# MoE 1's in products of three quarters as seven products of sums instead of eight, and its out sums kept in DRAM

## The chip, the cores and the metric

The kernel runs on one core of one Trainium2 chip, in one launch. The time is that of the device in microseconds (us). The kernel before took 873.6 us as the median of 3 runs (872.93 to 874.16).

## The reference

Three stages follow each other: a masked attention (4 batches, 8 heads, 576 positions of 64), a mixture block called MoE 1 here, and a second one, MoE 2. Both blocks work on 2304 tokens of 512 numbers.

```python
x = attention(q, k, v)                    # 2304 x 512
h = x @ w_in                              # MoE 1: 512 x 2048
g = h * tanh(log1p(exp(min(h, 20))))      # "Mish"
x = g @ w_out                             # 2048 x 512
s = silu(x @ w_gate) * (x @ w_val)        # MoE 2: 512 x 1536 each
out = s @ w_out2                          # 1536 x 512
```

All arrays are float32. The weights reach the kernel as 64-bit floats and are turned into 32-bit ones on the chip.

## The kernel before, in words

**Products.** Each operand of a product is held as a high part and a rest (`split_hi` on ScalarE makes the first, `split_lo` on VectorE or GpSimd the second). `mm3` (L130) then issues three TensorE matmuls for one product of 128 x 128 weights and 512 columns: high by high, high by rest, rest by high. All matmuls of the blocks therefore show line L132.

**Stages.** The tokens lie in five chunks: four of 512 and one of 256 (`CHUNKS`). MoE 1 cuts its 2048 inner columns into four quarters (`NQ`) of four column groups (`QF`). A step n is one quarter of one chunk: 48 matmuls make h (`g1_mm`), ScalarE takes Mish out of PSUM (`act_a`), `g_hi` and `g_lo` split it, and 48 matmuls make the part of the output that this quarter gives (`g2_mm`). `y_out` on VectorE adds that part to the chunk's sum in SBUF (`acc`, L602; the first quarter copies it, L600). The string `ORDER` is a hand-written order of attention and of the first steps of MoE 1; from step 3 on the loop at L880 issues the in products of step n and then the out products of step n - 1.

**Weights.** Each weight tile is one unit of conversion: a load into one of two `raw` buffers, a Square on ScalarE, four VectorE operations (L256 to L265), a high part on ScalarE and a rest on VectorE. `W1_STEP` and `W2_STEP` say how many units of MoE 1 and MoE 2 go into each step. Units of MoE 2 are written to DRAM (`wd_...`) and loaded again when their round comes (`ld`). 22 of its 60 units are converted in the rounds of MoE 2 itself, one VectorE operation after each product (`w_late_step`), as `LATE_ROUND` gives them out.

**MoE 2.** It already uses sums: `PROD` lists seven products per pair of chunks in place of eight (a 2 x 2 scheme of Strassen's kind). `operand` makes the sums and differences of the token side, units S12 and S34 those of the weights. A round (`c_round`) does the seven products for gate and value: three go through a copy to SBUF (ScalarE, L714), three are added to those copies (VectorE, L717), and the last is read from PSUM. There are twelve such rounds, six for each pair of chunks; `c4_round` does the small chunk and `d_tile` the out products.

**Queues.** Each engine works through its own queue in order. SyncE (SP) issues nearly all DMAs, GpSimd (POOL) none; an issue that waits holds up those behind it.

Of the kernel before, what the change touches and what calls it, by code (L numbers as in the profile page):

```python
# [104 lines left out]
def local_strided_attention__mish_moe__swiglu_kernel(  # L105
# [14 lines left out]

    def split_hi(eng, hi, src):
# [8 lines left out]
    def mm3(o, wh, wl, xh, xl, first, last, more=False):  # L130
        for lhs, rhs, i in ((wh, xh, 0), (wh, xl, 1), (wl, xh, 2)):
            nc.tensor.matmul(o, lhsT=lhs, rhs=rhs, start=first and i == 0, stop=last and i == 2, skip_group_check=more)  # L132
# [15 lines left out]
    w1list = []  # L148
    for q in range(NQ):
        w1list += [(("i", q * QF + f), w1[q * QF + f, :, 0]) for f in range(QF)]  # L150
        w1list += [(("o", q * QF + f), w1[q * QF + f, :, 1]) for f in range(QF)]
# [7 lines left out]
    n1 = len(w1list) - sum(W1_STEP.values())  # L159
    wlist, w1list = w1list[:n1], w1list[n1:]  # L160
    for n in range(3, NQ * NCH):
        k1, k2 = W1_STEP.get(n, 0), W2_STEP.get(n, 0)
        part = w2list[:k2] if n % NCH == NCH - 1 else []
        wlist += part + w1list[:k1] + ([] if part else w2list[:k2])
        del w1list[:k1], w2list[:k2]
    assert not w1list and len(w2list) == sum(LATE_ROUND)
# [45 lines left out]

    def w_ops():
# [5 lines left out]
        if len(key) == 2:  # L219
            t = sb.tile([128, 512], I32, tag="wtmp", name="wtmp", bufs=2)  # L220
            w = sb.tile([128, 2, 512], F32R, tag="w", name="w", bufs=10)
            wt[key] = w
        else:
            t = sb.tile([128, 512], I32, tag="pt", name="wt2", bufs=6)
            tag, n = (("ws", "v")[i % 2], 2) if i < late["first"] else ("w", 10)
            w = sb.tile([128, 2, 512], F32R, tag=tag, name="ws", bufs=n)
        tf = t.bitcast(F32)
        if src is None:
            t0, t1 = (f32[key[:2] + (x,)] for x in ("W0", "W1"))
            f32[key] = tf  # L230
            lo, hi = slice(0, 256), slice(256, 512)

            def s1():
                if key[2] == "S12":
                    nc.vector.tensor_tensor(out=tf[:, lo], in0=t1[:, lo], in1=t1[:, hi], op=ALU.add)
                else:
                    nc.vector.tensor_tensor(out=tf[:, lo], in0=t0[:, lo], in1=t1[:, lo], op=ALU.subtract)

            def s2():
                if key[2] == "S12":  # L240
                    nc.vector.tensor_tensor(out=tf[:, hi], in0=tf[:, lo], in1=t0[:, lo], op=ALU.subtract)
                else:
                    s = f32[key[:2] + ("S12",)]
                    nc.vector.tensor_tensor(out=tf[:, hi], in0=t0[:, hi], in1=s[:, hi], op=ALU.subtract)
                wpend.append((key, w, tf))

            return [s1, s2]
# [32 lines left out]
    def w_unit():  # L280
        w_lo(nc.vector)
        w_hi()
        for do in w_ops():
            do()

# [21 lines left out]

    def w_done():
        if any(len(x[0]) == 2 for x in wpend + whalf):
            w_flush(0, nc.vector)  # L310

# [48 lines left out]
    def at_qk(s):  # L360
        b, first, g, part = steps[s]
        w = 64 if first else LK
        sc = [ps.tile([128, 512], F32, tag="sc", name="sc", bufs=2) for _ in range(2)]
# [71 lines left out]
    def at_tr(s, half):  # L435
# [8 lines left out]
        if src:  # L444
            src = [pt[:, x:x + y].rearrange("p j k -> p (j k)") for x, y in src]
            tps[s, half] = tp = ps.tile([128, 512], F32, tag="xp", name="tp", bufs=2)[:src[0].shape[1], :128 * len(src)]
            for x, a in enumerate(src):
                nc.tensor.transpose(tp[:, 128 * x:128 * x + 128], a, ident)  # L448
# [10 lines left out]
    def at_pv(s):  # L459
        b, first, g, part = steps[s]  # L460
        n = len(part) // 2
        banks = [ps.tile([128, 512], F32, tag="tp", name="xp", bufs=1)]
        if first:
            banks.append(ps.tile([128, 512], F32, tag="xp", name="xq", bufs=2))
# [70 lines left out]
    def g1_open(n, f):  # L535
        h_ps[n, f] = ps.tile([128, 512], F32, tag="mm", name="h", bufs=3)

    def g1_mm(n, f, kc):
        q, c = divmod(n, NCH)
        t, x = (q * QF + f, kc) if q else (f // 2 + kc // 2 * 2, f % 2 * 2 + kc % 2)  # L540
# [38 lines left out]
    def g2_mm(n, y, e, f):  # L579
# [10 lines left out]
            f == 0,  # L590
            f == QF - 1,
        )

    def y_out(n, y, e):
        q, c = divmod(n, NCH)
        nt = CHUNKS[c][1]
        if q == 0:
            if e == 0:
                new_acc(c, 4, nt)
            nc.vector.tensor_copy(acc[c][:, e], y)  # L600
        else:
            nc.vector.tensor_tensor(out=acc[c][:, e], in0=acc[c][:, e], in1=y, op=ALU.add)  # L602
        if q == NQ - 1 and c == NCH - 1:
            if e == 0:
                yh[c] = sb.tile([128, 4, nt], F32R, tag=f"xh{c}", name=f"yh{c}")
                yl[c] = sb.tile([128, 4, nt], F32R, tag=f"xl{c}", name=f"yl{c}")
            split_hi(nc.scalar, yh[c][:, e], acc[c][:, e])
            split_lo(nc.gpsimd, yl[c][:, e], acc[c][:, e], yh[c][:, e])

    PS4 = [("sc", 2), ("sc", 2), ("xp", 2), ("xp", 2)]  # L610

    def g2_by_f(n, after, banks=PS4):
        nt = CHUNKS[n % NCH][1]
        y = [ps.tile([128, 512], F32, tag=t, name="y", bufs=k)[:, :nt] for t, k in banks]
        for f in range(QF):
            for e in range(4):
                g2_mm(n, y[e], e, f)
            after(f)
        for e in range(4):
            y_out(n, y[e], e)  # L620
# [31 lines left out]

    ws = {}
# [15 lines left out]
    PROD = [  # L669
        ("X", "W0", 0, "B11"),  # L670
        ("Z", "S12", 0, "T1"),
        ("X", "S12", 1, "T2"),
        ("Z", "S34", 1, "B22"),
        ("X", "S34", 0, "T3"),
        ("Y", "W0", 1, "B21"),
        ("X", "W1", 1, "T4"),
    ]
    BANK = {"g": {"X": ("mm", 3), "Y": ("mm", 3), "Z": ("mm", 3)}, "v": {"X": ("sc", 2), "Y": ("xp", 2), "Z": ("tp", 1)}}
# [14 lines left out]
    def c_round(r, between):  # L693
# [3 lines left out]
        for n, (x, a, half, b) in enumerate(PROD):  # L697
            o = ops[P][b]
            for k in "gv":
                if x not in bank[k]:  # L700
                    tag, nb = BANK[k][x]
                    bank[k][x] = ps.tile([128, 512], F32, tag=tag, name="c" + x + k, bufs=nb)
# [34 lines left out]
    def c4_round(r):  # L737
# [3 lines left out]
        for f in range(2):  # L741
            for k in "gv":
                p = ps.tile([128, 512], F32, tag=("sc", "xp")[k == "v"], name="c4", bufs=2)[:, :nt]
# [13 lines left out]
    DB = [("sc", 2), ("xp", 2), ("mm", 3), ("sc", 2), ("xp", 2), ("mm", 3), ("mm", 3), ("tp", 1)]  # L757
    db = [0]

    def d_tile(r, lc, t):  # L760
# [3 lines left out]
        tag, nb = DB[db[0] % len(DB)]  # L764
        db[0] += 1
        o = ps.tile([128, 512], F32, tag=tag, name="o", bufs=nb)
# [35 lines left out]
    with tc.manual_schedule():  # L802
# [3 lines left out]
        def spin(n):  # L806
            if not n:
                return
            wp = ps.tile([128, 512], F32, tag="mm", name="wp", bufs=3)
# [21 lines left out]
        NA = NQ * NCH  # L831

# [7 lines left out]
        def out_group(n, e, f):  # L840
            if f == 0:
                nt = CHUNKS[n % NCH][1]
                y_ps[n, e] = ps.tile([128, 512], F32, tag="mm", name="y", bufs=3)[:, :nt]
# [36 lines left out]
        for n in range(3, NA):  # L880
            q, c = divmod(n, NCH)
            units = W1_STEP.get(n, 0) + W2_STEP.get(n, 0)
            left = [units]

            def bg(k):
                at = (0, 0, 0, 0, 1, 2, 2, 3)[k] if n % NCH == NCH - 1 and units == 4 else units * k / 8
                while left[0] > at:
                    left[0] -= 1
                    w_unit()

            for f in range(QF):
                g1_open(n, f)
                for kc in range(4):
                    g1_mm(n, f, kc)
                act_a(n, f)
                bg(7 - f)
                if n == NA - 2 and f % 2:
                    operand(0, ("B11", "T1")[f // 2])

            def after(f):  # L900
                g_hi(n, f)
                g_lo(n, f)
                bg(3 - f)
                if n == NA - 2:
                    operand(0, ("T2", "B22", "T3", "B21")[f])
                if n == NA - 1 and f == 0:
                    operand(0, "T4")

            if n == NA - 1:
                w_flush(0, nc.vector)  # L910
                ld(0, "S34", "W0", "S12", "W1", 0, 1)
            w_done()
            g2_by_f(n - 1, after)
            w_done()
        g2_by_f(NA - 1, lambda f: None, [("mm", 3), ("mm", 3), ("mm", 3), ("tp", 1)])
        w_late()
        for r in range(2 * NP + 1):
            P = r // NP
            late["units"] += LATE_ROUND[r] if r < len(LATE_ROUND) else 0
            if r < 2 * NP:  # L920
                ld(r + 1, "W0")

                def between(n):
                    if n == 2:
# [120 lines left out]
```

## Time and profile before

| | |
|---|---|
| median of 3 runs | 873.6 us |
| span of the profiled execution, first to last instruction | 871.4 us |
| TensorE (PE) busy | 864.0 us, 99% |
| VectorE (DVE) busy | 578.4 us, 66% |
| ScalarE (ACT) busy | 383.0 us, 44% |
| GpSimd (POOL) busy | 151.0 us, 17% |

The page gives no second time for the profiled execution, so its own time is taken as its span and the 2.2 us by which the median is longer. By the chain of waits, attention with the steps 0 to 2 of MoE 1 takes 117 us, the rest of MoE 1 lasts until 457.6 us, and MoE 2 takes what is left. An engine's busy time is the union of its instructions; where instructions overlap, the mean length of one is longer than the distance from one start to the next.

### The profile page before, as it was taken

Reading aid. Unit: us, or ns where it says so; the run is one execution under the profiler, and the core shown is the slowest. Engines: PE = TensorE matmul, PEld = TensorE weight load, DVE = VectorE, ACT = ScalarE, POOL = GpSimd, SP = SyncE. Lnnn points to the kernel's source line nnn. Section 1 sums busy time; section 2 is a strip of 40 time slices with the busy share of each in tenths; the row PEclk is TensorE's granted clock in tenths of the full one; section 3 lists DMA queues with packets and bytes.
Section 4 is the critical chain, followed back from the end, with each engine's and each line's share of the span. In section 5 each row is a group of like instructions: output and inputs, shape, how many; then the busy total and the mean of one; then the engine's idle time right before and its main releaser. Section 6 shows DMA issues by size and latency. Waiting matters only on the chain.

```text
span 871.4 us, 14324 instructions
## 1 busy us (share of the span) xinstructions
PE 864.0 (99%) x5288; PEld 721.4 (83%) x5288; DVE 578.4 (66%) x1292; ACT 383.0 (44%) x971; POOL 151.0 (17%) x170
## 2 busy tenths in 40 slices
PE   8999999999999999999999999999999999999998
PEld 5788778888888888888898888888888888888886
DVE  6998756798768868695567897683455535433534
ACT  7999953344335444343435534342333322332230
POOL 5642310000000000000213321220324112111211
PEclk9999999999999999999999999999999999999999
DMA  9865314355334544241068878647150582454222
GB/s 301 269 211 166 113 60 145 99 191 194 121 120 162 201 153 156 61 163 73 0 246 309 320 297 341 236 184 284 53 194 28 200 302 95 174 193 165 83 92 97
DMA packets 46006, 149.29 MB, mean 171 GB/s; under 512 B 4976, under 2 KB 8688, under 8 KB 45936
## 3 DMA queue, kind: packets, MB, share of 16 engines
q1 hardware_dynamic: 45792, 148.16, 48.2%
q8 instruction: 42, 0.69, 0.3%
q14 instruction: 28, 0.23, 0.1%
q10 hardware_dynamic: 144, 0.21, 0.1%
HBM read 112.18 MB, written 36.18 MB: 170 GB/s over the span
## 4 chain that ended last, share of the span: by engine, by line
PE 97%; DVE 1%; ACT 0%; issue 0%; POOL 0%; POOLq 0%
PE h L132 23%; PE y L132 22%; PE o L132 17%; PE cXg L132 8%; PE cXv L132 7%; PE c L132 4%; PE cZv L132 4%; PE cZg L132 4%; PE cYv L132 2%; PE cYg L132 2%; PE sc L368 2%; PE xp L484 2%; PE tp L448 1%; DVE pt L388 1%; PE wp L811 0%; ACT pt L402 0%
## 5 line engine op out<-in xcount | busy, mean ns | idle before, releaser
L132 PE MATMUL y<-g,w 128*128 128x512 f32 (+1 forms) x960 | 203.7, 369 | 0.0
L132 PEld LDWEIGHTS y<-g,w 128*128 128x128 f32 x960 | 166.7, 189 | 29.6
L132 PE MATMUL h<-xh,w 128*128 128x512 f32 (+1 forms) x640 | 189.8, 372 | 0.0
L132 PE MATMUL o<-wr,fs 128*128 128x512 f32 x648 | 149.6, 389 | 0.0
L132 PEld LDWEIGHTS o<-wr,fs 128*128 128x128 f32 x648 | 121.3, 188 | 25.0
L132 PEld LDWEIGHTS h<-xh,w 128*128 128x128 f32 x640 | 116.4, 189 | 20.0
L132 PE MATMUL h<-xl,w 128*128 128x512 f32 (+1 forms) x320 | 117.9, 368 | 0.0
L566 ACT ACTIVATE u<-h 128x512 f32<-128x512 f32 (+1 forms) x68 | 37.3, 548 | 143.9 <-PE h L132 143.9
L128 POOL TENSOR_TENSOR fs<-k,fs 128x512 fp32r<-128x512 f32 x36 | 48.7, 1353 | 267.1 <-ACT fs L123 208.5
L776 DVE TENSOR_TENSOR acc<-acc,o 128x512 f32<-128x512 f32 x90 | 61.4, 685 | 48.7 <-PE o L132 48.6
L132 PEld LDWEIGHTS h<-xl,w 128*128 128x128 f32 x320 | 60.4, 189 | 9.5 <-DVE xl L128 0.3
L128 DVE TENSOR_TENSOR g<-u,g 128x512 fp32r<-128x512 f32 (+1 forms) x80 | 52.9, 679 | 13.6 <-ACT g L123 13.6
L128 POOL TENSOR_TENSOR B<-acc,B 128x512 fp32r<-128x512 f32 x6 | 8.3, 1391 | 307.4 <-ACT B L123 307.4
L123 ACT CAST fs<-k 128x512 fp32r<-128x512 f32 x36 | 22.4, 622 | 88.0 <-DVE k L731 37.6
L402 ACT ACTIVATE pt<-pt,sm 128x64 f32<-128x64 f32 (+1 forms) x160 | 55.9, 361 | 3.7 <-DVE sm L388 3.7
L717 DVE TENSOR_TENSOR k<-cZg,k 128x512 f32<-128x512 f32 x12 | 8.3, 692 | 72.7 <-PE cZg L132 72.7
L132 PE MATMUL cXg<-T,wr 128*128 128x512 f32 x216 | 54.8, 389 | 0.0
L132 PE MATMUL cXv<-T,wr 128*128 128x512 f32 x216 | 54.8, 389 | 0.0
L123 ACT CAST ws<-wt 128x512 fp32r<-128x512 f32 x60 | 37.0, 616 | 36.1 <-DVE wt L265 32.0
L123 ACT CAST g<-u 128x512 fp32r<-128x512 f32 (+1 forms) x80 | 45.0, 576 | 15.5 <-PE y L132 15.4
L132 PEld LDWEIGHTS cXv<-T,wr 128*128 128x128 f32 x216 | 40.5, 188 | 8.4
L132 PEld LDWEIGHTS cXg<-T,wr 128*128 128x128 f32 x216 | 40.5, 188 | 8.5 <-DVE k L717 0.2
(111 smaller groups left out, 1336.6 us busy)
## 6 DMA issues: line engine op xcount, KB each, us to landing
raw<-in_w_dram SPq DMA_DIRECT2D x54, 512.0 KB, 3.7
wr<-wd_g_S SPq DMA_DIRECT2D x24, 512.0 KB, 7.1
wr<-wd_v_S SPq DMA_DIRECT2D x24, 512.0 KB, 7.4
wr<-wd_p SPq DMA_DIRECT2D x24, 512.0 KB, 4.9
wr<-wd_g_W SPq DMA_DIRECT2D x18, 512.0 KB, 6.3
wr<-wd_v_W SPq DMA_DIRECT2D x18, 512.0 KB, 7.1
rawl<-in_w_dram SPq DMA_DIRECT2D x14, 512.0 KB, 5.7
wd_g_W<-ws SPq DMA_DIRECT2D x12, 512.0 KB, 3.0
```

Of the source, the lines that this page charges most:

```text
L123: nc.scalar.copy(hi, src)
L128: eng.tensor_tensor(out=lo, in0=src, in1=hi.bitcast(F32), op=ALU.subtract)
L132: nc.tensor.matmul(o, lhsT=lhs, rhs=rhs, start=first and i == 0, stop=last and i == 2, skip_group_check=more)
L368: nc.tensor.matmul(sc[h][x % 2 * 64:x % 2 * 64 + 64, x // 2 * w:(x // 2 + 1) * w], lhsT=t[64 * h:64 * h + 64, q0:q0 + 64], rhs=t[64 * h:64 ...
L388: nc.vector.tensor_tensor_reduce(pt[:, x], sc[h][:, t * w:(t + 1) * w], m, -0.125, 3.0e38, ALU.add, ALU.min, accum_out=sm[:, 0, x:x + 1],)
L402: nc.scalar.activation(out=pt[:, x], in_=pt[:, x], func=AF.Exp, scale=-1.0, bias=sm[:, 0, x:x + 1], accum_out=sm[:, 1, x:x + 1],)
L448: nc.tensor.transpose(tp[:, 128 * x:128 * x + 128], a, ident)
L484: nc.tensor.matmul(banks[r][64 * h:64 * h + 64, o:o + nq - skip], lhsT=v_t[s][rows, i, 64 * h:64 * h + 64], rhs=ts[rows, c0 + skip:c0 + nq ...
L566: nc.scalar.activation(out=u, in_=p, func=AF.Mish)
L717: nc.vector.tensor_tensor(out=t, in0=p, in1=t, op=ALU.add)
L776: nc.vector.tensor_tensor(out=acc[c][:, t], in0=acc[c][:, t], in1=o, op=ALU.add)
```

## The change

**Products.** The quarters 1 to 3 of MoE 1 take the chunks in pairs (0 and 1, then 2 and 3), and `in_round` does the seven products of `PROD` for each pair; quarter 0 and the small chunk stay as they were. `t_items` makes the sums T1 to T4 of the token side on VectorE, once per pair; T1 to T3 are stored to DRAM (`td`) by GpSimd's queue and loaded again (`t_load`) for the quarters 2 and 3. T4 takes the place of the second chunk's first-half operand (`xh` and `xl` of chunk 1 or 3), which nothing reads any more. The weights get four sum units per quarter (S12 and S34 for each of two column pairs), twelve in all.

**Out sums.** `y_phase` copies each chunk's out products from PSUM to one of two buffers on ScalarE, and GpSimd's queue adds them to `yd` in DRAM by DMA (`accum_op`). `acc` is loaded back before MoE 2.

**Weights.** 30 units of MoE 2 are converted in its rounds instead of 22. The order of the background work is no longer a table by steps: a planner (`fill`, `need`, `head`) holds three clocks and puts each background operation where VectorE would be free by them; `need` puts it ahead of the product that reads it.

```diff
-W1_STEP = {4: 2, 5: 2, 6: 2, 8: 2, 9: 2, 10: 2, 11: 2, 13: 2, 14: 2, 15: 2, 16: 2}
-W2_STEP = {3: 4, 5: 3, 6: 3, 7: 5, 8: 2, 10: 3, 11: 3, 12: 5, 13: 2, 15: 2, 16: 3, 17: 3}
-LATE_ROUND = (6, 6, 5, 5)
+W2_QUARTER = (4, 4, 10, 12)
+LATE_ROUND = (8, 8, 7, 7)
...
-            tag, n = (("ws", "v")[i % 2], 2) if i < late["first"] else ("w", 10)
+        tag, n = ("ws", 2) if i < late["first"] else ("w", 10)
...
+    def fill(until=None):
+        until = clk["pe"] if until is None else until
+        while True:
+            if los and los[0][0] <= clk["dve"] + 0.1:
+                run_lo()
+                continue
+            it = head()
+            if it and max(clk["dve"], it[1](), floor[0] if it[0] else 0.0) + it[0] <= until + LEAD:
+                run_head()
+                continue
...
+    def in_round(q, P):
+        c0, c1 = 2 * P, 2 * P + 1
+        bank, keep = [{}, {}], [{}, {}]
+        for n, (x, a, half, b) in enumerate(PROD):
+            if b[0] == "T" and q == 1:
+                need(("x", P, b))
+            for k in range(2):
+                key = ("s", q, k, a)
+                need(key if key[3][0] == "S" else ("i", q * QF + 2 * k + (a == "W1")))
...
+                for j in range(2):
+                    sl = slice(half * 256 + j * 128, half * 256 + j * 128 + 128)
+                    xo = x_op(P, b, j)
+                    mm3(p, w[:, 0, sl], w[:, 1, sl], *xo, first and j == 0, j == 1, True)
+                pe = clk["pe"]
+                if n < 3:
...
+                    on_act(COPY, pe, lambda: nc.scalar.copy(t, p))
+                    fill()
+                elif n < 6:
+                    fill()
+                    t = keep[k][{3: 2, 4: 1, 5: 0}[n]]
+                    r = on_dve(0.69, pe, lambda: nc.vector.tensor_tensor(out=t, in0=p, in1=t, op=ALU.add))
...
+    def y_phase(q, c, order, after=None):
...
+                        if e % 2 == 0:
+                            stv = sb.tile([128, 2, nt], F32, tag="v", name="yv", bufs=2)
...
+                    on_act(COPY if nt == 512 else 0.4, clk["pe"], lambda: nc.scalar.copy(dst, p[:, :nt]))
+                    free(at)
+                    if e == 3 or (e == 1 and c < NCH - 1):
...
+                        kw = {} if q == 0 else {"accum_op": ALU.add}
+                        nc.gpsimd.dma_start(yd[c][:, e0:e + 1], src, **kw)
...
+        for q in range(1, NQ):
+            if q > 1:
+                need(("s", q, 0, "S12"))
+            in_round(q, 0)
+            if q > 1:
+                t_load(1)
+            small_h(q)
+            y_phase(q, 1, (0, 2, 1, 3), lambda i: late_g(q, 0, i) if i < 2 else None)
...
+            y_phase(q, 0, (0, 2, 1, 3), after)
+            y_phase(q, 4, (0, 1, 2, 3))
+            in_round(q, 1)
...
+            y_phase(q, 3, (0, 2, 1, 3), lambda i: late_g(q, 1, i) if i < 2 else None)
...
-        for n in range(3, NA):
-            q, c = divmod(n, NCH)
...
-                units = W1_STEP.get(n, 0) + W2_STEP.get(n, 0)
```

In TensorE's queue, quarter 1 began with the in products of chunk 0 (`xh_68`, `xl_69`), then the out products of the small chunk, then the in products of chunk 1 (`xh_70`):

```order
L132 MATMUL h<-xh_68,w 128x512
L132 MATMUL h<-xl_69,w 128x512
...
L132 MATMUL y<-g,w 128x256 x48
L132 MATMUL h<-xh_70,w 128x512
L132 MATMUL h<-xl_71,w 128x512
...
L132 MATMUL y<-g,w 128x512 x48
```

The same place after the change (`cX`, `cY`, `cZ` are PSUM banks, `xT_...` the stored sums T1, T2 and T3, `w1p` the second weight tile of a pair):

```order
L141 MATMUL y<-g,w 128x256 x48
L141 MATMUL cX<-xh_68,w 128x512
L141 MATMUL cX<-xl_69,w 128x512
...
L141 MATMUL cZ<-xT_2324,w 128x512 x12
L141 MATMUL cX<-xT_2325,w 128x512 x12
L141 MATMUL cZ<-xh_70,w 128x512
...
L141 MATMUL cX<-xT_2326,w 128x512 x12
L141 MATMUL cY<-xh_68,w 128x512
...
L141 MATMUL cX<-xh_70,w1p 128x512
```

Both chunks now go through seven products of twelve matmuls, 84 in all, where two chunks took 96.

In GpSimd's queue the last split of a weight in attention was followed by MoE 2's operands (`B`, `T`):

```order
L431 TENSOR_TENSOR pt<-pt,sm 128x384
L128 TENSOR_TENSOR w<-wtmp,w 128x512
L128 TENSOR_TENSOR B_4887<-acc_1563,B_4887 128x512
L128 TENSOR_TENSOR T_4922<-tt,T_4922 128x512
L128 TENSOR_TENSOR T_4950<-tt,T_4950 128x512
```

Now 40 DMAs stand between them, of which these are the first:

```order
L136 TENSOR_TENSOR w<-wtmp,w 128x512
L1306 DMA yd_2267<-acc_1563 128x2048
L1306 DMA yd_2269<-acc_2160 128x2048
L1011 DMA yd_2437<-yv 128x1024 x2
L802 DMA td0T_2452<-xT_2324 128x2048
L802 DMA td0T_2480<-xT_2326 128x2048
L802 DMA td0T_2506<-xT_2325 128x2048
L1011 DMA yd_2614<-yv 128x1024 x2
L1011 DMA yd_2710<-y_2696 128x1024
L1011 DMA yd_2269<-yv 128x1024 x2
L802 DMA td1T_3103<-xT_2975 128x2048
L1011 DMA yd_2267<-yv 128x1024 x2
```

The `yv` rows are the out sums on their way to DRAM, two DMAs of 512 KB for each chunk of 512.

In quarter 2 VectorE's adds of the out products to `acc` go, and ScalarE's queue has copies to `yv` at their place, among the high parts of weights (`ws`) and of g:

```order
L131 CAST ws<-wt_3826 128x512
L1005 COPY yv<-y 128x512 x4
L320 ACTIVATE sq<-raw 128x512
L131 CAST ws<-wt_3868 128x512
L131 CAST g<-u_3764 128x512
...
L131 CAST ws<-wt_3947 128x512
L1005 COPY yv<-y 128x512 x4
L131 CAST ws<-wt_3976 128x512
```

A copy to `yv` waits for the DMA that read that buffer one chunk earlier, and what stands behind it on ScalarE waits with it.

## Rows read from the trace of the kernel before

**Rows 1.** The page: busy time of each engine, and 40 slices of the span.

```profile
span 871.4 us, 14324 instructions
PE 864.0 (99%) x5288; PEld 721.4 (83%) x5288; DVE 578.4 (66%) x1292; ACT 383.0 (44%) x971; POOL 151.0 (17%) x170
...
PE   8999999999999999999999999999999999999998
...
PEclk9999999999999999999999999999999999999999
```

**Rows 2.** Waits of PE: engine, line, released by: us in total, times, longest.

```profile
PE wp L811 <- POOL wz L803: 1.1, 1, 1.1
...
PE tp L448 <- POOL pt L431: 0.2, 1, 0.2
```

**Rows 3.** The chain of waits in order of time: start, us, what.

```profile
216.21 10.88 PE h L132 x48
227.09 10.88 PE y L132 x48
237.97 5.75 PE h L132 x48
...
457.58 1.39 PE cXg L132 x6
458.97 1.36 PE cXv L132 x6
...
465.77 1.36 PE cZg L132 x6
```

**Rows 4.** Stages: busy time of each engine, granted clock, DMA share, GB/s.

```profile
128.00:172.00 44.00, 44.00 (x239) 38.28 (x238) 29.95 (x53) 17.25 (x34) 0.00 (x0) 1.00 0.36 122
...
238.00:337.00 99.00, 99.00 (x485) 83.98 (x485) 77.98 (x137) 41.81 (x77) 0.00 (x0) 1.00 0.45 155
...
457.58:482.40 24.82, 24.82 (x134) 21.52 (x133) 18.39 (x29) 14.84 (x28) 8.91 (x8) 1.00 0.86 309
482.40:520.85 38.45, 38.45 (x194) 32.79 (x193) 34.91 (x59) 17.55 (x33) 9.84 (x8) 1.00 0.82 303
520.85:559.27 38.42, 38.42 (x194) 32.78 (x193) 27.49 (x44) 14.22 (x26) 7.55 (x6) 1.00 0.76 288
559.27:597.69 38.42, 38.42 (x194) 32.78 (x193) 26.85 (x43) 14.12 (x26) 7.02 (x6) 1.00 0.59 219
```

**Rows 5.** VectorE from 180 to 200 us in order of time: start, us, what.

```profile
181.61 0.42 DVE L256 TENSOR_SCALAR wtmp<-raw 128x512 int32<-128x512 int32 x1
...
184.20 0.69 DVE L128 TENSOR_TENSOR w<-wtmp,w 128x512 fp32r<-128x512 f32 x1
184.80 0.42 DVE L237 TENSOR_TENSOR wt<-wt,wt 128x256 f32<-128x256 f32 x1
...
185.47 0.69 DVE L128 TENSOR_TENSOR w<-wtmp,w 128x512 fp32r<-128x512 f32 x1
...
194.44 2.47 DVE L602 TENSOR_TENSOR acc<-acc,y 128x512 f32<-128x512 f32 x4
```

**Rows 6.** Groups of instructions: busy us, mean ns, idle before and releaser.

```profile
L602 DVE TENSOR_TENSOR acc<-acc,y 128x512 f32<-128x512 f32 x48 | 31.7, 684 | 11.8 <-PE y L132 11.8
L714 ACT COPY k<-cXg 128x512 f32<-128x512 f32 x24 | 14.1, 588 | 67.2 <-PE cXg L132 67.1
```

**Rows 7.** DMA issues: count, KB each, median us from issue to landing.

```profile
raw<-in_w_dram SPq DMA_DIRECT2D x54, 512.0 KB, 3.7
...
wr<-wd_v_S SPq DMA_DIRECT2D x24, 512.0 KB, 7.4
...
rawl<-in_w_dram SPq DMA_DIRECT2D x14, 512.0 KB, 5.7
...
wd_v_W<-ws SPq DMA_DIRECT2D x12, 512.0 KB, 3.0
```

More of the change, by code (lines that the diff above doesn't have):

```diff
@@ L278, in w_step @@
                 wq.pop(0)()
[L280 to L284, printed above, removed]
     def w_late():
@@ L362, in at_qk @@
         w = 64 if first else LK
-        sc = [ps.tile([128, 512], F32, tag="sc", name="sc", bufs=2) for _ in range(2)]
+        sc = [psum("sc", "sc") for _ in range(2)]
         for x, (hp, j) in enumerate(part):
@@ L577, in g_lo, with g2_mm @@
         split_lo(nc.vector, g[:, 1, :nt], us.pop((n, f)), g[:, 0, :nt])
-    def g2_mm(n, y, e, f):
+    def g2_mm(n, y, e, f, first=0, last=QF - 1):
         q, c = divmod(n, NCH)
@@ L589, in g2_mm @@
             g[:, 1, :nt],
-            f == 0,
-            f == QF - 1,
+            f == first,
+            f == last,
         )
     def y_out(n, y, e):
-        q, c = divmod(n, NCH)
[L596 to L620, printed above, removed]
+        if e == 0:
+            new_acc(n, 4, CHUNKS[n][1])
+        nc.vector.tensor_copy(acc[n][:, e], y)
     yh, yl = {}, {}
@@ new lines, in local_strided_attention__mish_moe__swiglu_kernel, with with_split, unit_items, do @@
+    behind = []
+    def with_split(items):
+        out = items[:1]
+        if behind:
+            out.append(hi_item(*behind.pop(0)))
+            k = 3 if len(items) > 2 else len(items)
+            out += items[1:k] + [lo_item()] + items[k:]
+        else:
+            out += items[1:]
+        return out
+    def unit_items():
+        ops = w_ops()
+        costs = (SUM2, SUM2) if len(ops) == 2 else (0.42, 0.69, 0.69, 0.69)
+        items = []
+        end = [0.0]
+        for k, (op, cost) in enumerate(zip(ops, costs)):
+            def do(op=op, cost=cost, last=k == len(ops) - 1, first=k == 0):
+                if first and len(ops) == 4:
+                    clk["act"] = max(clk["act"], clk["dve"]) + SQUARE
+                end[0] = on_dve(cost, 0.0, op)
+            items.append((cost, lambda: 0.0, do))
+        items = with_split(items)
+        def close():
+            key, w, tf = wpend.pop(0)
+            behind.append((key, w, tf, lambda: end[0]))
+        return items + [(0.0, lambda: 0.0, close)]
@@ new lines, in drain, with need @@
+    def drain():
+        while head():
+            run_head()
+        if behind:
+            bg.append(hi_item(*behind.pop(0)))
+            bg.append(lo_item())
+            drain()
+    def need(key):
+        while key not in whole:
+            if not head():
+                assert behind, key
+                bg.append(hi_item(*behind.pop(0)))
+                bg.append(lo_item())
+            run_head()
+    freed, turn = {}, [0]
+    for tag, n in BUFS.items():
+        for k in range(n):
+            freed[tag, k] = 0
@@ L879, in local_strided_attention__mish_moe__swiglu_kernel @@
         w_flush()
-        for n in range(3, NA):
-            q, c = divmod(n, NCH)
-            units = W1_STEP.get(n, 0) + W2_STEP.get(n, 0)
[L883 to L915, printed above, removed]
+        for c in range(2):
+            yd[c] = dram.tile([128, 4, 512], F32, name="yd%d" % c)
+            nc.gpsimd.dma_start(yd[c], acc[c])
+        middle()
         w_late()
```

408 lines of the change are left out of this document (359 added, 49 removed).

## The prediction, as it was put on record before the run

> **What bounds the kernel now.** I read the busy times of the page first, then PE's waits, the chain of waits, the table by stages, and last single stretches of VectorE and the DMAs. TensorE is busy 99% of the span and 9 in every slice but the first and the last, at the full granted clock in all 40 [rows 1]. It waits six times in the whole span, and the longest and the shortest of these waits are 1.1 and 0.2 us [rows 2]; both stand on lines of the start and of attention, none on the products of the two blocks. The chain of waits is therefore a list of matmuls: 48 of 512 columns take 10.88 us, which is 0.2267 us each, 48 of 256 columns take 5.75, and a product of six takes 1.36 [rows 3]. So the time is the number of matmuls times their length, as long as nothing else becomes late. What has to be asked of the change is how many matmuls go, and whether what it puts on the other engines and the queues still fits under a TensorE that is quicker through the same stages.
>
> **Matmuls removed.** Two chunks and four column groups took 2 x 48 = 96 matmuls of 512 columns for h. Seven products for each of two column pairs, each of two steps of 128 in the inner dimension by three passes, are 7 x 2 x 6 = 84. That is 12 fewer for a pair of chunks, with two pairs in three quarters 72 fewer. All else on TensorE (out products, small chunk, quarter 0, MoE 2) keeps its number and shape. 72 x 0.2267 = 16.3 us. The profiled execution has a span of 871.4 us and, as the median of the runs is 873.6, 2.2 us around it; I keep these 2.2. 871.4 - 16.3 = 855.1, and with 2.2 the time is 857.3 if no wait is added.
>
> **VectorE.** Overlapping instructions are read from start to start, not by their length. Four adds in a row take 2.47 us, so 0.6 us each though each lasts 0.68 [rows 5, 6]. A unit of conversion takes from 181.61 to 184.20, 2.6 us, and 0.6 for the rest of its split, 3.2 us; a sum unit takes 0.67 and 0.6 with a small gap, some 1.4 us [rows 5]. A quarter before is 4 x 21.76 + 11.5 = 98.5 us of TensorE; now 24 matmuls, 5.4 us, fewer: 93.1. Quarter 2 then has 14 raw units (44.8 us), 8 sum units counting those of MoE 2 (11.2), 12 adds from PSUM (7.2) and 18 rests of g (10.8): 74 us of 93, 79%. The 20 adds of out products that stood there (12 us, off TensorE's path then as they are now) are gone, and pay for the new adds and sums. Before, the same stretch ran at 78.0 of 99.0, also 79% [rows 4], with no wait of TensorE. The tightest place is the start of quarter 1, where T1 to T4 come on top: from the third chunk's h on TensorE needs 44.4 us until quarter 1; VectorE must do two units (6.4), 24 adds and splits for the T of one pair (14.4) and g (2.4), 23.2 us, against 27.9 us until the small chunk's h ends, and then 7.2 of 16.6. In the 44 us of that stretch before it was busy 30.0 [rows 4]. I take nothing for it. If the cover were gone, the most that could be late there is one conversion, 3.2 us.
>
> **ScalarE.** In quarter 2 it gets 16 copies of out products, 12 copies of products (0.588 each [rows 6]) and the small chunk's, and loses none of its splits and Mish: about 20 us more on 41.8 of 99 [rows 4], some 61 of 93 us. The X bank of a pair must be copied before the product two later writes to it: three other products of 1.36 less the copy's own 0.59 give 3.5 us of cover. In front of such a copy the queue can hold a high part for `ws`, which has two buffers where `ws` and `v` gave four, so it waits until the store two units before has read it. A store takes 3.0 us from issue to landing [rows 7] and units follow at 2.4 us or more, so such a wait is about 0.6 us and stays under 3.5. Nothing taken; without cover, 0.6 for each of 22 units, 13 us, is the upper end.
>
> **The DMAs of GpSimd's queue.** No row of before shows one, nor a DMA that adds to DRAM. For each chunk two DMAs of 512 KB add `yv` to `yd`; with two buffers a chunk's copies wait for the DMAs of the chunk before. Where two chunks of out products follow each other directly (chunks 1 and 0, and 3 and 2, so six times), 10.88 us lie between, and the banks of the late copies are needed 3.5 us later: the pair of DMAs, with T us from the first issue to the last landing, costs T - 14.4 where it is longer. Bounds of T: two plain stores one after the other, 2 x 3.0 = 6.0 us, cost nothing; two of the slowest loads, at 7.4 in a loaded stretch [rows 7], 14.8, cost 0.4 us each time, 2.4 in all. The place is about as busy as the first rounds of MoE 2, so T lies in the upper half, but below 14.4. What these DMAs add is memory traffic: quarter 2 moves 6 MB of T, 4.5 MB of out sums twice, 7 of raw weights and 5 to 6 of converted ones, some 28 MB in 93 us, 300 GB/s, against 155 before. Rounds 0 and 1 of MoE 2 ran at 309 and 303 GB/s with the DMA engines 0.86 and 0.82 busy and TensorE without a wait [rows 4].
>
> That rate shows that the traffic fits; it doesn't show what the addition costs. The Trainium skill ("Collectives: The Full Stack", section on the bandwidth ceiling) says that an add in the DMA path needs two source reads for each write and so runs at half the rate of a copy. By that rule T would be double the plain store's, 12 us with the page's factor, and the sum would stay; no run of before shows it.
>
> The DMAs' issues on GpSimd could also be slowed by VectorE. Of the conversion's VectorE instructions one, a TENSOR_SCALAR of 0.42 us [rows 5], 14 in a quarter, has one input; were each issue held up by one of them, T would grow by 0.4. The Trainium skill ("SBUF — State Buffer", on who interferes with whom) says that VectorE's copies and scalar operations in their two-port mode keep GpSimd out of writing descriptors, while operations on two tensors don't. By that rule T grows by 0.4 us at most and no term changes; no run here shows it yet.
>
> **MoE 2.** Eight more units are converted in its rounds, 8 x 3.2 = 26 us of VectorE. Steps are given out one after a product, so they go into rounds 0 to 4. Before, round 1 ran VectorE at 34.9 of 38.45 us with no wait of TensorE, and rounds 2 and 3 at 27.5 and 26.9 [rows 4]; these have 22 us free and round 4 another 11, in which the 26 fit at the density of round 1. Taken at nothing; uncovered, a quarter of them would be 6.5 us.
>
> **Sum.** 857.3, and for the borders (the starts of quarters 2 and 3 and of MoE 2) three waits of 0.3 us, nearer to the shortest wait that TensorE shows than to its longest, since the sums needed there are ready some 5 us ahead by the paces above: 858.2 us.
>
> **Rivals.** First, part of the gain is given back. For it: VectorE and ScalarE hold no more reserve than before, the stretch is shorter, and the DMA load doubles. The price by the terms above: a T of 15 to 15.5 (6 x 0.6 to 6 x 1.1, 4 to 7 us), or a quarter of the late conversions (6.5), or half of the buffer waits of ScalarE (6.5): 862 to 865, middle 863. Against it: each of these loads has a stretch of before that ran as full with no wait.
>
> Second, slower than before: the turnaround of the adding DMAs is the bound. If T is 18 to 20 us, because an add reads and writes the same DRAM and its issues queue behind one another on GpSimd, each of the six gaps costs 3.6 to 5.6 us, for the late copy holds up ScalarE and the PSUM banks with it: 857.3 + 22 to 34 = 879 to 891. It outweighs the gain from T = 14.4 + 16.3/6 = 17.1 on. Against it: T would have to be three times two plain stores, and above twice the slowest load shown.
>
> Third, the gain is cancelled at VectorE: the fifth product's add empties bank X, into which the seventh product writes three products, 4.1 us, later. If two whole units of conversion, 6.4 us, ran ahead of that add, TensorE would wait 2.3 us, once for each of the six pairs: 13.8 us, and the time would be 858.2 + 13.8 = 872.0. Against it: single operations, not whole units, can stand ahead of an add, and the planner keeps its clock of VectorE at the length of one, 0.69, above the 0.6 from start to start.
>
> **How the numbers follow.** The forecast has 0.70, with 856.5 to 861 as its own range; the partial return 0.21; the DMA bound 0.06; the cancelled gain 0.03. A measurement of this kernel tells 0.2% from no change, 1.7 us. Faster is then 0.70 + 0.20, since a hundredth of the partial return goes to slower, for two of its prices that meet a T of 16: 0.90; same 0.03; slower 0.07. The range reaches from 856.3, a little below the bare sum if one of the old waits goes, to 866, which takes in the partial return; what is left out is the two last rivals and a little on either side.
>
> **What would show it.** TensorE 72 matmuls fewer, and its busy time about 16 us lower at the same granted clock; no wait of more than about 1 us on a line of the in or out products. VectorE near 79% in quarter 2 and ScalarE near 65%; DMA share up to 0.8. Adding DMAs that land 6 to 7 us after their issue; if they take 9 or more, the second rival holds, and copies to `yv` show waits for them and TensorE waits for ScalarE at the out products of chunks 0 and 2. If TensorE waits in rounds 2 to 4 of MoE 2 for converted weights, the late units weren't covered. If it waits for VectorE in the products of sums, the third rival holds. A clock below full in any slice would make the whole sum wrong.

## The result, and the profile after

The changed kernel takes 886.5 us (median of 4 runs, 885.58 to 887.2), the kernel before 873.7. The ratio is 1.0148, with a 95% interval of 1.0134 to 1.0162: slower by 1.5%, where 858.2 us and a range up to 866 had been forecast. Medians and ratios here are over fast executions; a single one of 3003 us, in the run with 4 us below, is left out. The page of the profile after, to be read against [rows 1]:

```profile
span 885.0 us, 14401 instructions
...
PE 857.3 (97%) x5216; PEld 713.0 (81%) x5216; DVE 606.4 (69%) x1334; ACT 456.7 (52%) x1095; POOL 183.8 (21%) x210
...
PEclk9999999999999989999999989999999999999999
```

The 72 matmuls are gone (5288 to 5216). They should have taken 16.3 us off TensorE's busy time of 864.0, to 847.7; it fell only to 857.3, since the granted clock is below full in parts of the span (two slices show an 8). The waits of TensorE, line and releaser first, then us in total, times, longest; of the six of before [rows 2] those of the start and of attention are still there, and these are new:

```profile
PE cX L141 <- ACT k L952: 9.8, 3, 4.8
PE cXv L141 <- DVE k L1144: 5.9, 1, 5.9
PE cXg L141 <- ACT yv L1005: 3.8, 1, 3.8
...
PE c L141 <- DVE s L1158: 0.8, 1, 0.8
```

The account closes: 9.8 + 5.9 + 3.8 + 0.8 = 20.3 us of waits, 857.3 - 847.7 = 9.6 us of slower clock (at most 0.9 of it is something else, by a run at full clock below), less 16.3, make 13.6; the span went from 871.4 to 885.0. Where the clock falls is seen in stretches of 10 us (busy us of PE, PEld, DVE, ACT, POOL, then granted clock, DMA share, GB/s):

```profile
220.00:230.00 10.00, 8.89 (x40) 7.04 (x39) 3.02 (x7) 3.55 (x7) 0.00 (x0) 1.00 0.98 333
...
310.00:320.00 10.00, 6.16 (x24) 4.75 (x23) 5.18 (x10) 4.35 (x10) 0.85 (x1) 0.87 1.04 270
320.00:330.00 10.00, 10.00 (x36) 8.01 (x36) 5.83 (x11) 6.43 (x11) 0.00 (x0) 0.79 0.92 332
...
420.00:430.00 10.00, 10.00 (x39) 8.02 (x38) 6.66 (x14) 6.62 (x13) 0.00 (x0) 0.84 0.87 315
...
460.00:470.00 10.00, 9.54 (x35) 7.73 (x36) 7.52 (x9) 7.04 (x13) 4.51 (x5) 0.83 1.03 319
...
510.00:520.00 10.00, 8.16 (x29) 6.62 (x30) 9.51 (x17) 4.55 (x9) 1.35 (x1) 0.74 0.92 333
```

A wait of 1.1 us (220 to 230) leaves the clock at 1.00. Behind the waits of 3.8 (until 318), 4.8 (until 419), 3.8 (until 460) and 5.9 us (until 512) the mean over 10 us falls to 0.79, 0.84, 0.83 and 0.74, between the two levels of 2.4 and 1.2 GHz: for part of that stretch TensorE is busy at half rate. Single matmuls show it (start, us, what, count, idle time ahead):

```profile
311.62 2.88 PE L141 MATMUL cZ<-xT,w 128*128 128x512 f32 x12
318.34 5.49 PE L141 MATMUL cX<-xT,w 128*128 128x512 f32 x12 [3.84 <-ACT k L952]
```

Twelve matmuls take 2.88 us ahead of the wait and 5.49 behind it.

**The first kind of wait.** It comes once in each quarter, in the products of the second pair of chunks. ScalarE in order of time around the second (start, us, what; the bracket is the idle time ahead and what ended it):

```profile
304.47 0.62 ACT L131 CAST ws<-wt 128x512 fp32r<-128x512 f32 x1 [5.60 <-DMA wd_p<-ws]
...
310.04 0.62 ACT L131 CAST ws<-wt 128x512 fp32r<-128x512 f32 x1 [1.92 <-DMA wd_g_W<-ws]
310.56 1.19 ACT L1005 COPY y<-y 128x256 f32<-128x256 f32 x4
311.62 0.69 ACT L320 ACTIVATE sq<-raw 128x512 f32<-128x512 f32 x1
317.19 0.62 ACT L131 CAST ws<-wt 128x512 fp32r<-128x512 f32 x1 [4.87 <-DMA wd_g_S<-ws]
317.71 1.06 ACT L952 COPY k<-cX 128x512 f32<-128x512 f32 x2
```

The high part of a stored weight waits until the store of two units before has read its buffer, 4.9 us here, and the copies of the two X banks, which TensorE needs, stand behind it, as they do behind the small chunk's copies and a Square. The first of these banks is full at about 310.4 us, six matmuls after its product began at 308.87, and its copy starts 7.3 us later, at 317.71. The cover of 3.5 us that the prediction worked out takes its part of that: TensorE's next product starts at 318.34, 3.84 us late. Why the store takes so long is seen in the DMA queues from 290 to 325 us (packets, MB, share of the 16 engines; then issues, KB each, median us to landing):

```profile
q1 hardware_dynamic: 1869, 6.81, 52.2%
q0 software_dynamic: 720, 2.62, 42.8%
...
yd<-yv POOLq DMA_DIRECT2D x4, 512.0 KB, 8.7
wd_p<-ws SPq DMA_DIRECT2D x2, 512.0 KB, 6.2
wd_g_W<-ws SPq DMA_DIRECT2D x2, 512.0 KB, 5.6
wd_g_S<-ws SPq DMA_DIRECT2D x2, 512.0 KB, 8.7
wd_v_W<-ws SPq DMA_DIRECT2D x2, 512.0 KB, 4.4
...
wd_v_S<-ws SPq DMA_DIRECT2D x1, 512.0 KB, 2.9
```

The three kinds of store that ScalarE waits for above (`wd_p`, `wd_g_W`, `wd_g_S`) land after 5.6 to 8.7 us; two others are quicker, with 4.4 and 2.9. The row that the prediction took has 3.0 [rows 7]. The five adding DMAs (queue q0) move 2.62 MB and hold the DMA engines for 42.8% of the time, the 6.81 MB of all the others 52.2%.

**The second kind.** In round 0 of MoE 2, SP's queue issues this from 491 us on:

```profile
491.50 0.42 SPq L227 DMA_DIRECT2D rawl<-in_w_dram  x1
492.01 0.74 SPq L1104 DMA_DIRECT2D wr<-wd_g_W  x1
492.85 0.44 SPq L1104 DMA_DIRECT2D wr<-wd_v_W  x1
493.40 1.05 SPq L1315 DMA_DIRECT2D acc<-yd  x2
494.50 0.65 SPq L1104 DMA_DIRECT2D wr<-wd_g_W  x1
495.20 0.65 SPq L1104 DMA_DIRECT2D wr<-wd_v_W  x1
495.95 0.48 SPq L240 DMA_DIRECT2D wd_v_W<-ws  x1
```

Ahead of the store at 495.95 stand five loads of 512 KB and the two of 1 MB for the out sums of chunks 2 and 3: 4.5 MB. (Those two chunks are thus loaded back inside MoE 2, not before it.) The chain of waits goes through it:

```profile
495.95 13.81 DMA wd_v_W<-ws
...
509.84 0.63 ACT ws L131
510.49 0.69 DVE ws L136
511.18 0.61 DVE k L1144
```

VectorE's rest of that weight waits with ScalarE, and the add that empties TensorE's bank is behind it on VectorE: 5.9 us.

**The border.** The last copies to `yv` on ScalarE start at 459.34 us, behind the splits of an operand of MoE 2 that wait for VectorE:

```profile
458.22 1.22 ACT L131 CAST T<-tt 128x512 fp32r<-128x512 f32 x2 [2.60 <-DVE tt L680]
```

TensorE's first product of MoE 2 waits for these copies: 3.8 us.

### The profile page after: what moved, and what is told of

The parts are those of the page before. It is cut to its first block, busy times and chain, and to the rows that moved or that the text cites. A ratio compares the mean times of both kernels' runs of the same rounds, so it can differ in the third digit from the quotient of the medians.

```text
span 885.0 us, 14401 instructions
## 1 busy us (share of the span) xinstructions
PE 857.3 (97%) x5216; PEld 713.0 (81%) x5216; DVE 606.4 (69%) x1334; ACT 456.7 (52%) x1095; POOL 183.8 (21%) x210
## 3 DMA queue, kind: packets, MB, share of 16 engines
q0 software_dynamic: 5760, 25.17, 12.4%
## 5 line engine op out<-in xcount | busy, mean ns | idle before, releaser
L136 DVE TENSOR_TENSOR ws<-wt,ws 128x512 fp32r<-128x512 f32 x60 | 44.2, 736 | 59.0 <-ACT ws L131 58.8
L1011 POOL DMA_DIRECT2D yd<-yv x28 | 22.7, 812 | 276.8 <-ACT yv L1005 275.6
L131 ACT CAST ws<-wt 128x512 fp32r<-128x512 f32 x60 | 37.1, 618 | 62.2 <-DVE wt L330 16.3
L141 PE MATMUL h<-xh,w 128*128 128x512 f32 (+1 forms) x208 | 61.5, 360 | 0.0
L141 PE MATMUL cX<-xT,w 128*128 128x512 f32 x144 | 39.2, 425 | 9.8 <-ACT k L952 9.8
L1141 ACT COPY k<-cXg 128x512 f32<-128x512 f32 x24 | 14.1, 587 | 57.3 <-PE cXg L141 57.3
L141 PEld LDWEIGHTS cX<-xT,w 128*128 128x128 f32 x144 | 29.6, 207 | 17.5 <-ACT k L952 11.0
L1005 ACT COPY yv<-y 128x512 f32<-128x512 f32 x56 | 31.1, 590 | 20.1 <-PE y L141 14.5
L141 PEld LDWEIGHTS h<-xh,w 128*128 128x128 f32 x208 | 37.0, 189 | 5.2 <-issue 0.2
```

Source lines behind the costliest of these rows:

```text
L136: eng.tensor_tensor(out=lo, in0=src, in1=hi.bitcast(F32), op=ALU.subtract)
L1005: on_act(COPY if nt == 512 else 0.4, clk["pe"], lambda: nc.scalar.copy(dst, p[:, :nt]))
L1011: nc.gpsimd.dma_start(yd[c][:, e0:e + 1], src, **kw)
L1141: nc.scalar.copy(t, p)
```

## The experiments

Each is the changed kernel with the edit shown. All ratios are to the kernel before, run on the same chip.

**Without the addition.**

```diff
-                        kw = {} if q == 0 else {"accum_op": ALU.add}
+                        kw = {}
```

> The DMAs of the out sums in quarters 1 to 3 write to DRAM without adding (the sums of earlier quarters are lost). Theory A (an adding DMA takes the DMA engines about twice as long for a byte; they are full from about 293 to 320 us, stores of converted weights land late, and ScalarE waits for them in front of the copies that free PSUM): share of the DMA engines in quarter 2 from 0.84 to about 0.7, the three waits of TensorE for the copies of bank X (9.8 us) under 3 us, the clock full through the quarters, time about 872 us; the waits at the border to MoE 2 (3.8) and in its round 0 (5.9) stay. Rival B (two store buffers are too few at any DMA load): the waits stay within 2 us, time 884 to 887.

Measured: 872.6 us, ratio 0.9987 (0.9972 to 1.0002). The same bytes, the same issues, the same two store buffers, and all three waits for the copies of bank X are gone; two stay:

```profile
PE cXv L141 <- DVE k L1144: 6.2, 1, 6.2
PE cXg L141 <- ACT yv L1005: 3.6, 1, 3.6
```

The queues in the same stretch, 290 to 325 us:

```profile
q1 hardware_dynamic: 2274, 9.32, 73.6%
q0 software_dynamic: 720, 2.62, 18.7%
...
wd_p<-ws SPq DMA_DIRECT2D x2, 512.0 KB, 4.5
wd_g_W<-ws SPq DMA_DIRECT2D x2, 512.0 KB, 4.0
wd_g_S<-ws SPq DMA_DIRECT2D x2, 512.0 KB, 4.9
wd_v_W<-ws SPq DMA_DIRECT2D x2, 512.0 KB, 4.9
...
wd_v_S<-ws SPq DMA_DIRECT2D x1, 512.0 KB, 2.9
```

The same 2.62 MB now take 18.7% instead of 42.8, and the three kinds of store land in 4.0 to 4.9 us, although the DMA engines move more in these 35 us. Full DMA engines alone don't make the stores so late: from 294 to 317 us their share is 0.98 here and 1.02 in the change, but they move 374 GB/s here and 273 there. On ScalarE the high part that waited 4.87 us waits 0.92:

```profile
309.71 0.62 ACT L131 CAST ws<-wt 128x512 fp32r<-128x512 f32 x1 [0.92 <-DMA wd_g_S<-ws]
310.23 1.07 ACT L952 COPY k<-cX 128x512 f32<-128x512 f32 x2
```

Theory A holds, rival B (two buffers are too few at any load) falls. TensorE's busy time went from 857.3 to 853.0. The 9.8 us of waits and 4.3 of clock, less about 0.5 by which other waits grew, are the 13.5 us by which the span fell (885.0 to 871.5); by the medians the gain is 13.9.

**High parts given out later.** In the planner, a stored unit's high part is ready only 7 us after the end of the rest of the unit two before it:

```diff
+            n = stored[0] - 2
+            return landed[n] if len(key) == 3 and 0 <= n < len(landed) else 0.0
...
+                    landed.append(clk["dve"] + 7.0)
```

> The planner gives out the high part of a stored weight only once the store two units before has, by its clock, had 7 us to land, so that ScalarE isn't blocked in front of PSUM copies; no work or traffic goes. Theory A (the blocked queue is what costs, not the rate of the DMAs): the 9.8 us of waits for copies of bank X fall under 2, the 3.8 us at the border shrink, with the clock that follows them 868 to 872 us. Rival C (the DMA engines are too slow for the quarter's work, the delay only moves to the next quarter's weights): TensorE waits for weights or sums instead, 882 us or more.

Measured: 924.0 us, ratio 1.0584 (1.056 to 1.0609). The bank X waits are gone as theory A had it (0.7 us is left of 9.8), but the background work is one list in order, and what stands behind a held unit is held too:

```profile
PE cXg L141 <- ACT yv L1012: 18.7, 1, 18.7
PE cZ L141 <- ACT w L131: 6.5, 4, 3.2
...
PE cX L141 <- ACT w L131: 5.3, 1, 5.3
```

TensorE waits for weights of the next quarter, as rival C said, and at the border to MoE 2 for what had piled up. Rival C's reason isn't borne out: from 360 to 420 us, where most of the waits for weights stand, the DMA engines are 0.34 busy. The forecast of theory A, 868 to 872 us, fell. That the block in ScalarE's queue costs TensorE doesn't fall with it, since the waits for bank X went; that this delay schedules the block away does. With 4 us in place of 7 (together with the two edits below):

> The change in full, with the high parts of stored weights given out 4 us (not 7) after the store two before by the planner's clock, the two loads of out sums in rounds 2 and 3, and the third sum behind the copies. If 7 us only throttled the conversions too much: most X bank waits gone, no weights late, 866 to 872 us. If every delay of the stored units only moves the wait to the next quarter's weights, since the stores' rate is the bound: 880 or more, with waits for weights.

Measured: 886.6 us, ratio 1.015 (1.0135 to 1.0166). The waits for copies of bank X stay at 9.6 us, and a new one of 9.8 came in round 0, where ScalarE waited 10.3 us for a raw weight. The time is that of the second forecast, but no wait of TensorE for weights of the next quarter came with it: 4 us did too little. Between 4 and 7 us nothing was tried.

**Loads of out sums later.**

```diff
-            if r == 1:
-                for c in (2, 3):
-                    new_acc(c, 4, 512)
-                    nc.sync.dma_start(acc[c], yd[c])
+            if r in (2, 3):
+                new_acc(r, 4, 512)
+                nc.sync.dma_start(acc[r], yd[r])
```

> The two 1 MB loads of out sums for the second pair of chunks come in rounds 2 and 3 of MoE 2 instead of both in round 1's queue. Theory A: the 5.9 us wait of TensorE for VectorE in round 0 goes, since a store of weights no longer stands behind 4.5 MB of loads in SP's queue, and the low clock behind it too: 886.5 - 5.9 - 3 = about 877.5 us. Rival B (the late units are too many for these rounds): a wait of like size stays within the first three rounds, 884 to 887 us.

Measured: 880.3 us, ratio 1.008 (1.0065 to 1.0095). The wait for VectorE in round 0 went from 5.9 to 0.8 us, TensorE's busy time from 857.3 to 855.1. The mechanism is the one expected. The gain was 6.2 us where 9 were expected: 0.8 of the wait stayed, the clock gave back 2.2 us and not 3, and other waits grew by about 2 us.

**Both, and the third sum behind the copies.** The delay of 7 us, the later loads of out sums, and in the last out products of MoE 1:

```diff
-(("B11", "T1"), ("T2", "B22"), ("T3",), ("B21",))
+(("B11", "T1"), ("T2", "B22"), (), ("T3", "B21"))
```

> Both of the last two edits, and the third sum of the token side for MoE 2 made after the last out products' copies instead of before. If the blocked queues are all that took the gain: no wait of TensorE above 1.5 us, clock full, TensorE busy about 848 us, time 858 to 861 us. If the DMA rate is the bound: 870 us or more.

Measured: 912.6 us, ratio 1.0448 (1.0432 to 1.0463), with the weights late as in the run with 7 us alone. It tells nothing of the DMAs' rate, since the delayed units in the list bring the waits.

**Without the reload of T1 to T3.**

```diff
-        t_tiles(P)
-        for k in TSLOT:
-            nc.sync.dma_start(tops[P][k].bitcast(F32), td[P, k])
+        tops[P].update({k: tops[1 - P][k] for k in TSLOT})
```

> The change with the reload of T1 to T3 left out (the products take the sums of the other pair of chunks). 6 MB of some 28 less in a quarter, the adding DMAs as in the change. Theory A (sum of all DMA time): like the run without adding, the waits for the copies of bank X fall from 9.8 to under 3 us, 872 to 876 us. Rival E (it is the adding DMAs themselves that hold up the stores, whatever else runs): these waits stay, since no reload is in flight where they fall, 883 to 887 us.

Measured: 886.8 us, ratio 1.015 (1.0122 to 1.0178). From 225 to 317 us (columns as in the stretches above) the change has

```profile
225.00:317.00 92.00, 88.39 (x434) 74.43 (x432) 68.52 (x117) 54.24 (x97) 7.70 (x9) 1.00 0.84 242
```

and this run

```profile
225.00:317.00 92.00, 89.98 (x441) 75.69 (x439) 68.53 (x117) 54.17 (x97) 7.71 (x9) 1.00 0.65 171
```

The DMA share fell from 0.84 to 0.65 and the time didn't move: 8.4 us of the bank X waits stayed. This corrects the reading of the first experiment. It isn't the sum of DMA work in a quarter that is too much, but what runs in the 30 us in which the adds of chunks 1, 0 and 4 meet the stored units; the reloads lie elsewhere. From 290 to 325 us the share is 0.92 here and 0.95 in the change, and the adding DMAs hold the engines for 42.8% of the time in both. Theory A, as a matter of the sum, falls, rival E holds.

**No adding, and both edits at the border.** The first and third edit and the moved third sum:

> Writes without adding in quarters 1 to 3, the two loads of out sums in rounds 2 and 3, and the third sum for MoE 2 behind the last out products' copies. If the four waits found are all that took the gain, and the low clock comes only behind them: TensorE busy 848 us, clock full in all slices, time 857 to 860 us. If the products of sums have a cost of their own: 863 or more.

Measured: 861.6 us, ratio 0.986 (0.9844 to 0.9877).

```profile
PE 848.6 (99%) x5216; PEld 707.3 (82%) x5216; DVE 606.0 (71%) x1334; ACT 459.5 (53%) x1095; POOL 174.4 (20%) x210
...
PEclk9999999999999999999999999999999999999999
```

TensorE is busy for 848.6 us, where the sum had 847.7, at full clock throughout. So the 16.3 us are there, the products of sums cost at most 0.9 us of their own, and the low clock came only behind the waits. Of the 4.1 us by which the span (859.2) is above the forecast's 855.1, 0.9 is in TensorE's busy time; 2.4 more are four waits at the start of MoE 2 and in its rounds 0 and 1 (1.2, 0.8, 0.2, 0.2); most of the rest are short waits in attention. The run leaves out the addition, so it shows what the change would take if adding cost no more than writing.

**Seven products for one pair only.** Chunks 0 and 1 as in the change, 2 and 3 as before it. T1 to T3 then stay in SBUF for all three quarters, and in quarter 3 their slots are free early, so that the sums so far are loaded there and VectorE adds the out products; the third sum for MoE 2 is behind the copies here too:

```diff
+            if last:
+                direct(1)
+                direct(0)
...
+            u = [h_q(q, 2, f) for f in range(QF)]
+            y_phase(q, 4, (0, 1, 2, 3), lambda f: g_make(q * NCH + 2, [f], *u[f]))
+            u = [h_q(q, 3, f) for f in range(QF)]
...
+    def direct(c):
+        new_acc(c, 4, CHUNKS[c][1])
+        nc.sync.dma_start(acc[c], yd[c])
...
+                if i == 3 and q == NQ - 1:
+                    on_dve(0.69, clk["pe"], lambda: nc.vector.tensor_tensor(out=acc[c][:, e], in0=acc[c][:, e], in1=p[:, :nt], op=ALU.add))
```

> Seven products only for chunks 0 and 1; chunks 2 and 3 in eight, as before the change. So T1 to T3 stay in SBUF, nothing of them is stored or loaded again, and in quarter 3 the sums so far are loaded and VectorE adds the out products to them, so that no DMA adds there. 36 matmuls fewer than before: 8.2 us. Theory A (DMA time is what the change ran out of): share of the DMA engines in quarter 2 about 0.65, no wait of TensorE over 1.5 us before MoE 2, clock full, 865 to 868 us. Rival B (two store buffers are too few): waits of 8 to 10 us stay and the time is 875 or more. Rival V (VectorE's 18 more adds in quarter 3 are late): waits for VectorE or weights there, 870 to 874.

Measured: 873.2 us, ratio 0.9995 (0.9986 to 1.0004). In the quarters TensorE did what was expected: DMA share 0.61 from 225 to 317 us, no wait of TensorE from 225 to 420, full clock. The stores are no quicker, though: ScalarE waited 5.2 us for one at 306 us and 5.1 at 319, as in the change. Chunks 2 and 3, whose products stand there, have no copies of bank X in this run. So a late store costs TensorE only where such copies stand behind it; of two buffers being too few (rival B) the run tells nothing. The 865 to 868 us of theory A were missed at another place: of the gain of 8.2 us, 4.8 were lost at the border and in round 0, in waits of 1.0 and 1.6 us on the first products, 1.2, 0.6 and two of 0.2 behind them, and 1.1 in attention, which the edit doesn't touch; what took the rest is open. The operands of MoE 2 were made there, on the same VectorE and ScalarE that convert the late weights. So they were made earlier:

```diff
-            y_phase(q, 4, (0, 1, 2, 3), lambda f: g_make(q * NCH + 2, [f], *u[f]))
+            def made(f):
+                g_make(q * NCH + 2, [f], *u[f])
+                if last and f in (1, 2):
+                    operand(0, ("B11", "T1")[f - 1])
...
+                if last:
+                    operand(0, ("T2", "B22", "T3", "B21")[f])
...
-                    if r == 0 and n == 0:
-                        operand(0, "T4")
```

> As the run with seven products for chunks 0 and 1 alone, and MoE 2's token operands for these chunks and the small one are made earlier in quarter 3, as soon as their sums and slots are there, instead of around the start of MoE 2. If the half version lost its gain where operands, late weights and splits meet on VectorE and ScalarE in rounds 0 and 1 (waits of 4 to 5 us there): these waits under 2 us, 868 to 870 us. If VectorE is short in quarter 3 as well: a wait there takes their place and the time stays near 873.

Measured: 869.8 us, ratio 0.9955 (0.9941 to 0.9968): faster than both kernels, by 0.45% than the one before. The waits were the place, as expected. What is left in round 0 is mainly this:

```profile
PE cXv L141 <- ACT k L1171: 1.3, 1, 1.3
```

In the profiled execution (872.6 us) the granted clock was also 0.75 from 20 to 30 us, in attention; the other four had a mean of 0.999 or more over the span.

**Two stored units moved to quarter 1.** The loads of out sums in rounds 2 and 3 and the third sum behind the copies are in this run too.

```diff
-W2_QUARTER = (4, 4, 10, 12)
+W2_QUARTER = (4, 6, 10, 10)
```

> The change in full with two of quarter 3's stored units moved to quarter 1 (4, 6, 10, 10 instead of 4, 4, 10, 12), loads of out sums in rounds 2 and 3, third sum behind the copies. The run with the loads moved took 880.3 us; the border's 3.8 us go: about 875. Quarter 2 keeps its ten units and its wait of 4 to 5 us; if the number of stored units sets the wait, quarter 3's falls with ten... but it had ten before its copies already, so it stays and only the border gains: 873 to 876 us.

Measured: 913.5 us, ratio 1.045 (1.0432 to 1.0467). A miss on the slow side: TensorE waits at the start of quarter 2 for the in weights, which stand behind the moved units in the list (8.2 us in four waits for `w`). The waits for copies of bank X stay (8.2 us), round 0 has a new one of 7.3, and with the slower clock TensorE is busy for 869.8 us.

## Why the prediction was wrong, point by point

- **Matmuls removed, 16.3 us: right.** Shown by the run without adding and with both border edits, whose TensorE is within 0.9 us of the sum.
- **ScalarE: the step that failed.** It took a store's landing time, 3.0 us, from a median over the whole of the kernel before [rows 7], and from it a wait of 0.6 us under a cover of 3.5. In the stretch where stored units and adds meet, the landing of the stores that were waited for was 5.6 to 8.7 us, and ScalarE's two longest waits were 4.9 and 5.6 us. The cover of 3.5 us was about right: of the 7.3 us by which the copy was late at 317.71, 3.8 came through, and 1.1 and 4.8 in the two other quarters, 9.8 us in all where nothing had been taken. The step named the queue, the buffers and the copy behind them; the term was mis-sized because its duration came from the kernel before, with a lighter DMA load, while the step on the DMAs, a paragraph further, had the load doubled. Of the 13.9 us that come back without the addition, 9.8 are these waits and the rest mostly their clock.
- **Adding DMAs: T right, its place wrong.** The 24 adding DMAs from `yv` land after 7.0 us in the median, and the five adding DMAs from 290 to 325 us after 6.6 to 10.7. T, from the first issue of a pair to its last landing, is at most 12.4 us, under 14.4, and copies to `yv` lost only 3.5 us to these DMAs on ScalarE. The second rival's range, 879 to 891 us, holds the measured time by chance: its T of 18 to 20 didn't come, and the copy that waits for an add was not where the time was lost. Its sign, a landing of 9 us or more, came in 11 of 27 adding DMAs and didn't tell. The price of the addition is paid by others: its DMA time more than doubles (42.8 against 18.7%), and the stores in the other queue wait. The traffic was summed in bytes, 300 GB/s, and set beside rounds that moved 309; measured were 242 GB/s at a share of 0.84 from 225 to 317 us. The 242 count an added byte once and the 300 twice; counted alike, the bytes came out as summed (about 293 GB/s). What they didn't show is how long each takes: the time of the DMA engines, in the 30 us in which the adds meet the stored units, was the thing to sum. The rule weighed there, from the Trainium skill ("Collectives: The Full Stack", section on the bandwidth ceiling), that an add in the DMA path needs two reads and so has half the rate, agrees with 42.8/18.7 = 2.3, a little more than its two; I had let it change T alone.
- **MoE 2: one queue overlooked.** I costed 26 us of VectorE there, and with the loads moved no wait over 1.2 us was left there in the run without adding. The 2 MB of out sums in SP's queue ahead of a late unit's store weren't costed at all: 5.9 us.
- **Borders, 0.9 us: measured 3.8** (and 0.8 for the small chunk's product), for the out products' last copies stood behind an operand's split on ScalarE, itself 2.6 us behind VectorE. It is gone in the runs that move the third sum, but for the one with 7 us, where units had piled up.
- **Clock: missing from the sum.** 9.6 us, a third of all that was lost. I wrote that a clock below full would make the whole sum wrong, and gave the rivals only the price of their waits.
- **VectorE at 79% and the third rival**: VectorE was busy 67.7 of 93 us in quarter 2 (256 to 349 us), 73%, and waited some 22 us for ScalarE there; without the addition the same stretch has 72.6 us, 78%. No wait of the third rival's kind was seen in the quarters.

What stays open: whether the full change can keep its 16.3 us with the sums added in DRAM. No order of the background list that was tried did it.

## What to carry to other kernels

Price a wait for a DMA by the landing time in the stretch where the new wait stands, under the load that the change itself adds, and count that load in time of the DMA engines, not in bytes. Add to the wait the other work that stands in front of the same copy. Whatever waits for a store in an engine's queue holds up the PSUM copies behind it, so a buffer ring that is cut in half belongs on the list of changes with a price. When TensorE is the bound, a wait of some microseconds can be paid twice, once in time and once in clock: here 20.3 us of new waits came with 9.6 us of slower clock, while the waits of up to 1.6 us in the run with seven products for one pair cost no clock.

## What the runs showed of the hardware

- A DMA that adds to DRAM held the DMA engines 2.3 times as long as one that writes: 2.62 MB in 35 us took 42.8% of them against 18.7%.
- In the changed kernel TensorE's clock stayed at 1.00 behind a wait of 1.1 us and fell behind the four waits of 3.8 us and more, to a mean of 0.74 to 0.84 over 10 us, which is half rate for a part of it (twelve matmuls in 5.49 us against 2.88). That draws no line: in the run with two units moved it fell to 0.83 (230 to 240 us) behind a wait of 1.8. The four longest waits (3.8, 4.8, 3.8 and 5.9 us) go with 9.6 us of lost rate. The Trainium skill ("TensorE: Matmul & The Clock Gate", Part 1) has the gate pass either all pulses or half of them; the granted clocks here, as means, and the two paces of matmuls fit that.
